# Attention and two feed-forward layers on one core: q in six loads per chunk, k and v loads and score products spread, a new cost table for the list scheduler

## The chip, the cores and the metric

The kernel runs on one core of one Trainium2 chip. The metric is device time in microseconds (us), the median of the runs shown, lower is better. One profiled execution, with its trace, stands beside the runs. In the trace PE is TensorE's matrix engine and PEld its weight loads, ACT is ScalarE, DVE is VectorE, POOL is GpSimd, and SP is the queue that issues every DMA of this kernel (SPq in the rows).

## The reference, cut to what matters

```python
# q, k, v: (4 batches, 12 heads, 448 tokens, 64); w_pre, w_post: (12, 12)
scores = scale * np.matmul(q, k.transpose(0, 1, 3, 2))
scores = np.einsum('bhij,hg->bgij', scores, w_pre)         # mixes the heads
attn = np.exp(scores - np.max(scores, axis=-1, keepdims=True))
attn = attn / (np.sum(attn, axis=-1, keepdims=True) + 1e-09)
attn = np.einsum('bhij,hg->bgij', attn, w_post)            # mixes them again
x = np.matmul(attn, v)                                     # -> (1792 tokens, 768)
h = x @ w_in                                               # 768 -> 2048, then a gate
x = gate(h) @ w_out                                        # 2048 -> 768
h = x @ w_in2                                              # 768 -> 1024
out = layer_norm(h * softmax(h)) * g_ln @ w_out2           # 1024 -> 768
```

## The kernel before

The attention is cut into 16 chunks: 4 batches, and in each batch 4 chunks of 110, 110, 110 and 118 tokens. A chunk has 11 or 12 groups of 10 tokens (`GR`), and two groups make a pair, so there are 180 groups and 90 pairs. The same steps run for each chunk:

- `load_q` (L262) brings the chunk's q of all 12 heads into one of two slots of `qb`, with two DMAs. `load_k` (L255) brings k of two heads, six loads for a batch, and `load_v` (L271) brings v in four loads for a batch. A k tile lives in the ring `kraw`, of 12 buffers.
- `qk` (L282), six times, makes the scores of two heads in two tiles of the PSUM ring `psa` (4 tiles). It is the "score product" of the title.
- `qk_evac` (L290), twelve times on ACT, copies one head's scores to a tile `s`, from a ring of 5.
- `remap` (L295), twelve DMAs issued by SP, moves a tile `s` so that in `sr` a group's 10 tokens of all heads lie on the partitions. The buffer of `s` is free again when its remap has landed.

For each pair of groups follow `pre` (L306, PE, mixes the heads), `rmax` (L311, DVE), `expo` (L316, ACT, the exponential), `guard`, `norm` and `wscale` (L323 and L331 on POOL, L327 on DVE, the divisor folded into the mixing weights `wr`), `post` (L345, PE, 64 matmuls, mixes and transposes) and two copies to `at` (L361 on ACT or L363 on DVE). After a chunk's last pair `av` (L374, PE) runs twice, a copy and an addition follow (L383, L389), and `store_x` (L393) writes to the scratch `xs`. When the last remap is done, SP begins to load the weights of the first feed-forward layer (L547); their conversion on DVE, ACT and POOL and the first matmuls overlap the end of the attention.

The program is written out once, in the order that a planner makes on the host (class `Order`). Every step is a task with an engine, an assumed duration, dependencies, buffers of rings and a priority in units of groups. The planner walks through time: of the tasks of an engine that could start, it takes the one with the lowest priority number:

```python
            t = min((t for t in avail[e] if ready(t) <= st), key=lambda t: (t.prio, t.i))
```

On the chip only the order on each engine is left of it: every engine works off its own row in that order and waits at the head of it for what the task needs. SP is such a row too: a remap whose `s` is not ready holds up every load behind it. The priorities come from the table `OFFS`, added to the first group of a chunk (`t0`) or of a pair (`p`): `qk0` and `qks` place the score products, `sq` the q loads, `sk` the k loads, `sv` the v loads, `pre`, `rmax`, `expo`, `post`, `av0` the steps of a pair. The list `gates` adds a lower bound: a load in it comes no earlier in the planner's order than the `pre` of a given pair (`marks`).

Of the kernel before, what the change touches and what calls it, by code (L numbers as in the profile page):

```python
# [17 lines left out]
H, S, D = 12, 448, 64  # L18
# [4 lines left out]
T0 = [0, 110, 220, 330]  # L23
NTOK = [110, 110, 110, 118]
JC, JP = 4, 112
OFFS = dict(split=-7.944, pre=0.954, rmax=-3.67, expo=-5.22, guard=-3.381, norm=-0.14, post=2.988, eh=-16.359, el=-2.885, av0=11.716, avs=2.48, sq=-16.055, exact=174, sld=1000, linact=(), wral=0, early=18, b_in=984, b_x=988, b_out=991, b_x1=998, lw=-90, shal=180, wrp=(), vlp=(),
   qk0=-13.451, qks=0.797, dmalat=2100, sk=-4.076, sv=-8.254, nv=1, svs=0.624,
   mw=-5, start=(('k', 0, 1), ('q', 0, 1), ('k', 1, 1), ('q', 1, 2), ('k', 2, 2), ('q', 3, 3), ('k', 4, 2)))


BUFS = dict(kraw=12, q=2, vv=2, s=5, sr=2, p=8, st=8, wr=6, x=3, psa=4, psb=4)
LAT_DMA = 2100
XPOOL = (0, 1, 'in', 'out')
SCALE = {}
# [164 lines left out]
def attention(nc, od, pl, q, k, v, w_pre, w_post, mask, xs):  # L199

    P = OFFS
    add = od.add
# [195 lines left out]
    gates, marks = [], []  # L398
# [8 lines left out]
    def make_av(i, b, c, t):  # L407
        for u in range(2):
            pr = t + P['av0'] + P['avs'] * u
            m = add("PE", 2260, pr, av, i, b, c, u, deps=evs[i] + vt_d[b], new=[r_psa, r_psa], use=[(r_vv, b)])  # L410
            a1 = add("Activation", 370, pr, av_copy, i, c, u, deps=[m], new=[r_x], use=[(r_psa, -1)])
            a2 = add("DVE", 410, pr, av_add, i, c, u, deps=[a1], use=[(r_x, -1), (r_psa, -2)])
            avs.setdefault(i, []).append(m)
            stores[b].append(od.dma("SP", 625, 630, pr, store_x, i, b, c, u, deps=[a2], use=[(r_x, -1)]))

    def make_two(two):
        p = two[0][3]
        rms = two[0][5] + two[1][5]
        m = add("PE", 754, p + P['pre'], pre, [(tt, i, g) for i, b, c, tt, g, _ in two], deps=[t_w] + rms + t_zs[0] + t_zs[1],
                new=[r_psb, r_psb], use=[(r_sr, i) for i in sorted({x[0] for x in two})])  # L420
        marks.extend([m, m])
        x1 = add("DVE", 531, p + P['rmax'], rmax, p, deps=[m], new=[r_st], use=[(r_psb, -2)])
        y1 = add("DVE", 531, p + 1 + P['rmax'], rmax, p + 1, deps=[m], use=[(r_st, -1), (r_psb, -1)])
        x2 = add("Activation", 611, p + P['expo'], expo, p, deps=[x1], new=[r_p], use=[(r_psb, -2), (r_st, -1)])
        y2 = add("Activation", 611, p + 1 + P['expo'], expo, p + 1, deps=[y1], new=[r_p], use=[(r_psb, -1), (r_st, -1)])
        x3 = add("Pool", 165, p + P['guard'] - 5, guard, p, deps=[x2, y2], use=[(r_st, -1)])
        x3 = add("DVE", 80, p + P['norm'], norm, p, deps=[x3], use=[(r_st, -1)])
        x4 = add("Pool", 350, p + P['norm'], wscale, p, deps=[x3], new=[r_wr], use=[(r_st, -1)])
        m = add("PE", 912, p + P['post'], post, p, deps=[x4], new=[r_psb, r_psb], use=[(r_p, -2), (r_p, -1), (r_wr, -1)])
        same = two[0][0] == two[1][0]  # L430
        ends = []
        for k, (i, b, c, tt, g, _) in enumerate(two[:1] if same else two):
            if g == 0:
                for j in (i - 2,):
                    busy[i] = avs.get(j, [])
            for r in range(2):
                eng = "Activation" if (p // 2 + r) % 2 in EV else "DVE"
                n = 2 if same else 1
                dur = 500 if same else 300
                e1 = add(eng, dur + (60 if eng == "DVE" else 0), p + P['el'], evac, p, eng, r, k, n, i, g,  # L440
                         deps=[m] + busy.get(i, []), use=[(r_psb, -2 + r)])
                evs.setdefault(i, []).append(e1)
            if tt + n - 1 == last[i]:
                ends.append((i, b, c, last[i] + 1))
        for e in ends:
            make_av(*e)
# [3 lines left out]
    for i, (b, c) in enumerate(chunks):  # L450
        t0 = t
        n = GR[c] * R
        last[i] = t + GR[c] - 1
        if i == 0:
            q0 = {}
            for what, h0, nh in P['start']:
                if what == 'k':
                    for p in range(h0, h0 + nh):
                        kt[b, p] = od.dma("SP", 450, 640, -100, load_k, b, p, new=[r_kraw])
                else:  # L460
                    a1 = od.dma("SP", 1250, nh * 400, -100, load_q, i, b, c, h0, nh,
                                **(dict(join=[r_q]) if h0 else dict(new=[r_q])))
                    for h in range(h0, h0 + nh):
                        q0[h] = a1
        else:
            a1 = od.dma("SP", 1250, 2000, t0 + P['sq'] - 3, load_q, i, b, c, 0, H // 2, new=[r_q])
            gates.append((a1, t0 + P['sq'] - 3))
            q0 = {p: a1 for p in range(H // 2)}
        rms = []
        for h in range(H):  # L470
            pr = t0 + P['qk0'] + P['qks'] * h
            if c == 0 and b and h % 2 == 0:
                kt[b, h // 2] = od.dma("SP", 450, 640, pr + P['sk'] - 2, load_k, b, h // 2, new=[r_kraw])
                gates.append((kt[b, h // 2], pr + P['sk'] - 2))
            if h % 2 == 0:
                a1 = add("PE", 754, pr, qk, i, b, c, h // 2, deps=[q0[h // 2], kt[b, h // 2]], new=[r_psa, r_psa],
                         use=[(r_q, i), (r_kraw, b * H // 2 + h // 2)])
            a2 = add("Activation", 424, pr, qk_evac, b, c, h, deps=[a1], new=[r_s], use=[(r_psa, -1 if h % 2 else -2)])
            rms.append(od.dma("SP", 625, 550, pr, remap, i, b, c, h, deps=[a2], use=[(r_s, -1)],
                              new=[] if h else [r_sr], join=[r_sr] if h else []))  # L480
        if c == 0:
            vt_d[b] = []
            for m in range(4):
                pr = t0 + P['sv'] + m
                a1 = od.dma("SP", 450, 960, pr - 2, load_v, b, m, **(dict(join=[r_vv]) if m else dict(new=[r_vv])))
                gates.append((a1, pr - 4 if b else t0 + m))
                vt_d[b].append(a1)
        for g in range(GR[c]):
            pend.append((i, b, c, t + g, g, rms))
            if len(pend) == 2:  # L490
                make_two(pend)
                pend = []
        t += GR[c]
    for x, slot in gates:
        if slot >= 0:
            x.issue.deps.append(marks[min(int(slot), len(marks) - 1)])
    late = list(od.tasks)
    early = [u for n in A_EARLY for us in rg[n].users for u in us]

# [522 lines left out]
```

## Time and profile before

| | |
|---|---|
| median of 3 runs | 1160.25 us (1158.41 to 1170.82) |
| profiled execution, device time | 1163.11 us |
| span of its trace | 1161.3 us |
| mean granted TensorE clock | 0.973 |
| PE busy over the span | 1080.2 us (93%) |
| DVE, ACT, POOL busy | 675.2, 523.2, 300.6 us |

The span is the time from the first to the last instruction of the profiled execution; 1.8 us of its device time lie outside. Busy times of different engines overlap. The attention fills the span up to about 390 us, with its last pairs mixed into the first matmuls of the feed-forward layer; the two layers fill the rest.

### The profile page before, as it was taken

The numbers are of one execution on the slowest core, as the hardware profiler recorded it, in microseconds if no ns is written. First come the engines' busy times: TensorE is split into PE (matmuls) and PEld (weight loads), VectorE is DVE, ScalarE is ACT, GpSimd is POOL, SyncE is SP. The second block draws the span as 40 slices with busy tenths as digits, with TensorE's granted clock in tenths as the row PEclk, the third lists the DMA queues.
The fourth block names the chain that finished last, engine by engine and source line by source line (L and its number), as shares of the span: only waits on it lengthen the run. The fifth ranks groups of instructions, "written<-read, shape, count | busy, mean of one in ns | idle before, by whom it ended". The sixth has DMA issues, their size and how long they took to land.

```text
span 1161.3 us, 31401 instructions
## 1 busy us (share of the span) xinstructions
PE 1080.2 (93%) x13528; PEld 918.0 (79%) x13528; DVE 675.2 (58%) x1078; ACT 523.2 (45%) x1053; POOL 300.6 (26%) x427
## 2 busy tenths in 40 slices
PE   5897998988897889999999899899999999999998
PEld 1475775766676668998989799798999898998988
DVE  0453554545454997488887778688866534243241
ACT  2775776867675656422233222232334232232232
POOL 3111110111111684243444344354510000000000
PEclk7998999999999899999999999899999999999999
DMA  5766457546646451241423232333222000000001
GB/s 144 202 180 182 126 164 204 158 140 179 183 137 203 124 181 65 73 136 55 139 79 128 82 109 97 107 107 112 82 86 93 26 14 28 28 14 28 28 14 41
DMA packets 84514, 124.20 MB, mean 107 GB/s; under 512 B 31544, under 2 KB 71960, under 8 KB 84376
## 3 DMA queue, kind: packets, MB, share of 16 engines
q1 hardware_dynamic: 84376, 122.20, 34.6%
q8 instruction: 106, 1.74, 0.7%
q14 instruction: 32, 0.26, 0.1%
HBM read 66.17 MB, written 17.30 MB: 72 GB/s over the span
## 4 chain that ended last, share of the span: by engine, by line
PE 64%; DVE 16%; DMA 8%; POOL 4%; issue 3%; ACT 3%; SPq 1%; ACTq 0%; POOLq 0%; DVEq 0%
PE ps_post L345 7%; DMA sr<-s 5%; PE ps_qk L282 5%; PE ps_pre L306 4%; PE ps_av L374 4%; PE ps_o L704 4%; PE ps_o L706 4%; PE ps_o L705 4%; PE ps_h L674 4%; PE ps_h L676 4%; PE ps_h L675 4%; PE ps_ot L904 3%; PE ps_ot L902 3%; PE ps_ot L903 3%; PE ps_h L842 3%
## 5 line engine op out<-in xcount | busy, mean ns | idle before, releaser
L345 PEld LDWEIGHTS ps_post<-wr,p 64*64 64x64 f32 x5760 | 115.2, 142 | 55.9 <-issue 42.2
L704 PE MATMUL ps_o<-g,wout 128*128 128x448 f32 x384 | 144.8, 377 | 14.6 <-DVE x2acc L714 12.0
L345 PE MATMUL ps_post<-wr,p 64*64 64x60 f32 x5760 | 121.9, 228 | 35.6 <-issue 19.3
L706 PE MATMUL ps_o<-g,wout 128*128 128x448 f32 x384 | 143.8, 375 | 0.0
L705 PE MATMUL ps_o<-g,wout 128*128 128x448 f32 x384 | 143.7, 374 | 0.0
L311 DVE TENSOR_REDUCE nm<-ps_pre 128x1 f32<-128x448 f32 x180 | 102.1, 618 | 60.5 <-PE ps_pre L306 58.9
L290 ACT ACTIVATE s<-ps_qk 119x448 f32<-119x448 f32 (+1 forms) x192 | 97.4, 550 | 69.4 <-DMA sr<-s 50.7
L316 ACT ACTIVATE p<-ps_pre,nm 128x448 f32<-128x448 f32 x180 | 112.3, 635 | 27.9 <-DVE nm L311 27.7
L282 PE MATMUL ps_qk<-kraw,qb 64*64 64x448 f32 (+2 forms) x768 | 109.0, 589 | 16.8 <-ACT s L290 9.5
L593 POOL TENSOR_TENSOR m<-m,v 128x768 f32<-128x768 f32 (+1 forms) x52 | 95.2, 1831 | 89.2 <-DVE v L575 76.8
L714 DVE TENSOR_TENSOR x2acc<-ps_o,x2acc 128x448 f32<-128x448 f32 x168 | 100.3, 616 | 21.8 <-PE ps_o L706 21.5
L565 ACT ACTIVATE v<-v,ebias 128x768 int32<-128x768 int32 (+1 forms) x52 | 46.1, 887 | 131.9 <-DVE v L561 131.8
L306 PE MATMUL ps_pre<-sr,wp 64*64 64x448 f32 (+1 forms) x720 | 94.8, 557 | 3.0 <-ACT s L290 1.0
L374 PEld LDWEIGHTS ps_av<-at,vv 64*64 64x64 f32 x2688 | 80.3, 133 | 18.9 <-issue 7.9
L704 PEld LDWEIGHTS ps_o<-g,wout 128*128 128x128 f32 x384 | 73.5, 191 | 24.9 <-DVE x2acc L714 14.9
L848 DVE TENSOR_REDUCE st<-ps_h 128x1 f32<-128x1024 f32 x14 | 17.1, 1225 | 128.7 <-PE ps_h L844 128.7
L374 PE MATMUL ps_av<-at,vv 64*64 64x110 f32 (+1 forms) x2688 | 84.8, 259 | 6.6 <-ACT s L290 2.5
L323 POOL TENSOR_SCALAR nm<-nm 128x2 f32<-128x2 f32 x90 | 18.6, 207 | 278.3 <-ACT p L316 277.8
L363 DVE COPY at<-ps_post 128x480 f32<-128x480 f32 (+1 forms) x98 | 59.4, 612 | 38.8 <-PE ps_post L345 38.1
L680 ACT ACTIVATE t<-ps_h,half 128x448 f32<-128x448 f32 x64 | 40.3, 629 | 91.3 <-PE ps_h L676 87.9
L706 PEld LDWEIGHTS ps_o<-g,wout 128*128 128x128 f32 x384 | 73.7, 192 | 7.4
L705 PEld LDWEIGHTS ps_o<-g,wout 128*128 128x128 f32 x384 | 73.7, 192 | 7.0
(110 smaller groups left out, 2302.9 us busy)
## 6 DMA issues: line engine op xcount, KB each, us to landing
sr<-s SPq DMA_DIRECT2D x144, 192.5 KB
raw<-in_moe_w_out_dram SPq DMA_DIRECT2D x24, 768.0 KB
raw<-in_moe_w_in_dram SPq DMA_DIRECT2D x16, 768.0 KB
sr<-s SPq DMA_DIRECT2D x48, 210.0 KB
raw<-in_moe_w_in_dram SPq DMA_DIRECT2D x12, 512.0 KB
kraw<-in_k_dram SPq DMA_DIRECT2D x24, 224.0 KB
out_dram<-ot SPq DMA_DIRECT2D x13, 384.0 KB
vv<-in_v_dram SPq DMA_DIRECT2D x12, 384.0 KB
```

The lines of the kernel that those rows point to most:

```text
L282: nc.tensor.matmul(out=qk_t[b, c, 2 * p + e][64 * j:at_], lhsT=qb[rows, i % 2, lo:hi], rhs=kraw_t[b, p][rows], start=True, stop=True,)
L290: nc.scalar.activation(out=s[:n], in_=qk_t.pop((b, c, h))[:n], func=AF.Copy, scale=0.125)
L306: nc.tensor.matmul(out=pre_t[t][o:o + 64], lhsT=wp[k_], rhs=sr[i % 2][k_, g, :], start=True, stop=True)
L311: nc.vector.tensor_reduce(nm_t[t // 2][:, 0, t % 2:t % 2 + 1], pre_t[t], axis=AX.X, op=ALU.max, negate=True)
L316: nc.scalar.activation(out=p, in_=pre_t.pop(t), func=AF.Exp, bias=nm[:, 0, e], accum_out=nm[:, 1, e])
L345: nc.tensor.matmul(out=ps[i][64 * j:64 * j + 64, e, m, :], lhsT=p[64 * i:64 * i + 64, x:x + 64], rhs=wr[64 * i:64 * i + 64, e], start=True ...
L374: nc.tensor.matmul(out=ps[r][64 * j:64 * j + 64, a, :n], lhsT=v_t[b][rows, m, (h0 + j) * D:(h0 + j + 1) * D], rhs=at[rows, i % 2, m, h0 + ...
L593: nc.gpsimd.tensor_tensor(out=m, in0=m, in1=vt.pop(key).bitcast(F32)[:, :n], op=ALU.mult)
L704: nc.tensor.matmul(out=ps, lhsT=wh, rhs=g[:, 0], start=(i == 0), stop=False)
L705: nc.tensor.matmul(out=ps, lhsT=wh, rhs=g[:, 1], start=False, stop=False)
L706: nc.tensor.matmul(out=ps, lhsT=wl, rhs=g[:, 0], start=False, stop=(i == 1))
L714: nc.vector.tensor_tensor(out=dst, in0=op.pop((u, m)), in1=dst, op=ALU.add)
```

## The change

- `load_q` is called six times per chunk, each for two heads (a pair of DMAs of one head's rows each), at priorities `sq + sqs * p`, where it was called once. The first chunk's loads are as they were.
- The k loads of later batches get priorities of their own, `sk + sks * p`, counted from the chunk's first group, and so do the v loads (`sv + svs * m` with a step of 2.5); the v loads of the first batch move to priorities 1 to 7.
- The score products join the list `gates`: product p of a chunk comes no earlier in the planner's order than the pair at `t0 + qg + qgs * p`.
- The ring `kraw` has 8 buffers for 12.
- The planner's durations change: a remap has 800 and 1300 ns (issue and transfer) for 625 and 550, a pair of q DMAs 1200 and 380 where the whole load had 1250 and 2000, k and v loads 500 and 720 or 1150 for 450 and 640 or 960, `av` 2320 for 2260, `post` 945 for 912, `wscale` 390 for 350, the copy after `av` 335 for 370. Several offsets in `OFFS` change with them.

No step of the computation is added or left out, and the instructions on PE, ACT, DVE and POOL are the same in number. SP issues 12 DMAs for a chunk's q where it issued 2.

```diff
-OFFS = dict(split=-7.944, pre=0.954, rmax=-3.67, expo=-5.22, guard=-3.381, norm=-0.14, post=2.988, ...
-   qk0=-13.451, qks=0.797, dmalat=2100, sk=-4.076, sv=-8.254, nv=1, svs=0.624,
+OFFS = dict(sqs=1.5, sks=-5.148, qg=-14.0, qgs=1.359, split=-7.944, pre=0.481, rmax=1.193, expo=-8.093, ...
+   qk0=-13.451, qks=0.569, dmalat=2100, sk=-25.042, sv=-9.216, nv=1, svs=2.5,
...
-BUFS = dict(kraw=12, q=2, vv=2, s=5, sr=2, p=8, st=8, wr=6, x=3, psa=4, psb=4)
+BUFS = dict(kraw=8, q=2, vv=2, s=5, sr=2, p=8, st=8, wr=6, x=3, psa=4, psb=4)
...
-            a1 = od.dma("SP", 1250, 2000, t0 + P['sq'] - 3, load_q, i, b, c, 0, H // 2, new=[r_q])
-            gates.append((a1, t0 + P['sq'] - 3))
-            q0 = {p: a1 for p in range(H // 2)}
+            q0 = {}
+            for p in range(H // 2):
+                pq = t0 + P['sq'] + P['sqs'] * p
+                q0[p] = od.dma("SP", 1200, 380, pq, load_q, i, b, c, p, 1, **(dict(join=[r_q]) if p else dict(new=[r_q])))
+                gates.append((q0[p].issue, pq))
...
-                kt[b, h // 2] = od.dma("SP", 450, 640, pr + P['sk'] - 2, load_k, b, h // 2, new=[r_kraw])
-                gates.append((kt[b, h // 2], pr + P['sk'] - 2))
+                pk = t0 + P['sk'] + P['sks'] * (h // 2)
+                kt[b, h // 2] = od.dma("SP", 500, 720, pk, load_k, b, h // 2, new=[r_kraw])
+                gates.append((kt[b, h // 2].issue, pk))
...
+                gates.append((a1, t0 + P['qg'] + P['qgs'] * (h // 2)))
...
-            rms.append(od.dma("SP", 625, 550, pr, remap, i, b, c, h, deps=[a2], use=[(r_s, -1)],
+            rms.append(od.dma("SP", 800, 1300, pr, remap, i, b, c, h, deps=[a2], use=[(r_s, -1)],
...
-                pr = t0 + P['sv'] + m
-                a1 = od.dma("SP", 450, 960, pr - 2, load_v, b, m, **(dict(join=[r_vv]) if m else dict(new=[r_vv])))
-                gates.append((a1, pr - 4 if b else t0 + m))
+                pr = t0 + P['sv'] + P['svs'] * m if b else 1 + 2 * m
+                a1 = od.dma("SP", 500, 1150, pr, load_v, b, m, **(dict(join=[r_vv]) if m else dict(new=[r_vv])))
+                gates.append((a1.issue, pr))
```

What the table and the gates do to the order is shown at three places. The first is SP's row at the start, from the first chunk's remaps (`sr<-s`) on; `qb` is q. Before:

```order
L295 DMA sr<-s 10x11x448 x5
L262 DMA qb<-in_q_dram 64x6x110 x2
L295 DMA sr<-s 10x11x448 x13
L271 DMA vv<-in_v_dram 128x768 x3
L271 DMA vv<-in_v_dram 64x768
L295 DMA sr<-s 10x11x448
```

After, on the same engine from the same remaps on:

```order
L295 DMA sr<-s 10x11x448 x5
L262 DMA qb<-in_q_dram 64x110 x2
L295 DMA sr<-s 10x11x448 x2
L262 DMA qb<-in_q_dram 64x110 x2
L295 DMA sr<-s 10x11x448 x3
L262 DMA qb<-in_q_dram 64x110 x2
L295 DMA sr<-s 10x11x448 x2
L262 DMA qb<-in_q_dram 64x110 x4
L295 DMA sr<-s 10x11x448
L262 DMA qb<-in_q_dram 64x110 x2
L295 DMA sr<-s 10x11x448 x3
L271 DMA vv<-in_v_dram 128x768
```

The pairs of q loads and the first batch's v loads now stand between the remaps. Up to the second chunk's last remap, the 24th, SP's row holds 4 DMAs for q before and 20 after.

The second place is SP's row where the first batch ends: the 12-group remaps (10x12x448) are those of its last chunk, and `kraw` is k of the second batch. Before:

```order
L295 DMA sr<-s 10x12x448 x4
L255 DMA kraw<-in_k_dram 128x448
L393 DMA xs<-x 128x3x110
L262 DMA qb<-in_q_dram 64x6x110 x2
L255 DMA kraw<-in_k_dram 128x448
L295 DMA sr<-s 10x12x448 x3
L255 DMA kraw<-in_k_dram 128x448
L295 DMA sr<-s 10x12x448
L393 DMA xs<-x 128x3x110
L255 DMA kraw<-in_k_dram 128x448 x2
L295 DMA sr<-s 10x11x448 x3
L255 DMA kraw<-in_k_dram 128x448
```

After, from the second batch's second k load on (its first stands three remaps ahead):

```order
L255 DMA kraw<-in_k_dram 128x448
L295 DMA sr<-s 10x12x448
L262 DMA qb<-in_q_dram 64x120 x2
L255 DMA kraw<-in_k_dram 128x448 x2
L295 DMA sr<-s 10x12x448 x3
L262 DMA qb<-in_q_dram 64x110 x2
L255 DMA kraw<-in_k_dram 128x448 x2
L393 DMA xs<-x 128x3x110
L262 DMA qb<-in_q_dram 64x110 x2
L295 DMA sr<-s 10x12x448 x2
L393 DMA xs<-x 128x3x110
L295 DMA sr<-s 10x12x448
```

Before, the last k load stood behind three remaps of the batch that needs it. Now all six stand ahead of the fifth remap of the last chunk of the batch before. The v loads, which began two remaps behind the last k load, now begin 13 remaps behind it.

The third place is ACT's row at the same boundary: `s<-ps_qk` is the evacuation of one head's scores, `p,nm<-ps_pre,nm` the exponential of one group, `at<-ps_post` a copy behind `post`. Before:

```order
L290 ACTIVATE s<-ps_qk 119x448 x2
L383 ACTIVATE x<-ps_av 128x3x110
L316 ACTIVATE p,nm<-ps_pre,nm 128x448
L361 ACTIVATE at<-ps_post 128x2x48x5
L316 ACTIVATE p,nm<-ps_pre,nm 128x448
L290 ACTIVATE s<-ps_qk 119x448 x3
L316 ACTIVATE p,nm<-ps_pre,nm 128x448 x4
L290 ACTIVATE s<-ps_qk 119x448
L383 ACTIVATE x<-ps_av 128x3x110
```

After:

```order
L316 ACTIVATE p,nm<-ps_pre,nm 128x448 x2
L361 ACTIVATE at<-ps_post 128x2x48x5
L290 ACTIVATE s<-ps_qk 124x448 x2
L361 ACTIVATE at<-ps_post 128x2x48x5
L290 ACTIVATE s<-ps_qk 124x448
L316 ACTIVATE p,nm<-ps_pre,nm 128x448 x2
L361 ACTIVATE at<-ps_post 128x2x48x5
L290 ACTIVATE s<-ps_qk 124x448 x2
L316 ACTIVATE p,nm<-ps_pre,nm 128x448 x2
L290 ACTIVATE s<-ps_qk 124x448
L383 ACTIVATE x<-ps_av 128x3x110
```

Where three evacuations stood in a row with four exponentials behind them, one or two evacuations now alternate with one pair's two exponentials.

## Rows read from the trace of the kernel before

**Rows 1.** Busy us (and instructions) of PE, PEld, DVE, ACT, POOL; PEclk, DMA share, GB/s.

```profile
30.00:390.00 360.00, 316.37 (x9284) 238.06 (x9279) 181.65 (x385) 257.09 (x650) 55.92 (x177) 0.96 0.60 169
```

**Rows 2.** PE's waits between 30 and 390 us: total us, times, longest.

```profile
PE ps_post L345 <- issue: 18.9, 17, 4.3
PE ps_post L345 <- ACT p L316: 13.5, 12, 3.7
```

**Rows 3.** PE's timeline at three batch boundaries: start, us; idle before in brackets.

```profile
99.68 0.86 PE L345 MATMUL ps_post<-wr,p 64*64 64x60 f32 x44 [1.60 <-issue]
...
104.58 1.73 PE L282 MATMUL ps_qk<-kraw,qb 64*64 64x448 f32 x16 [1.55 <-DMA sr<-s]
...
113.09 3.73 PE L345 MATMUL ps_post<-wr,p 64*64 64x60 f32 x126 [3.03 <-ACT p L316]
...
185.21 0.98 PE L282 MATMUL ps_qk<-kraw,qb 64*64 64x448 f32 x8 [1.63 <-DMA kraw<-in_k_dram]
...
203.94 0.33 PE L345 MATMUL ps_post<-wr,p 64*64 64x60 f32 x4 [3.50 <-ACT p L316]
...
300.13 0.33 PE L345 MATMUL ps_post<-wr,p 64*64 64x60 f32 x4 [3.72 <-ACT p L316]
```

**Rows 4.** The chain that ended last, start, us, what: the start and two boundaries.

```profile
14.29 3.43 DMA sr<-s
...
102.48 9.20 DMA sr<-s
...
290.47 8.25 DMA sr<-s
```

**Rows 5.** Busy time by stretch, columns as in rows 1, around the boundaries.

```profile
113.00:116.60 3.60, 3.46 (x124) 3.31 (x128) 1.31 (x4) 2.76 (x8) 1.16 (x4) 0.55 0.58 197
189.70:191.60 1.90, 1.90 (x134) 1.90 (x131) 0.82 (x2) 0.99 (x3) 0.94 (x3) 1.00 0.70 206
197.50:203.90 6.40, 2.72 (x88) 2.25 (x82) 1.75 (x4) 2.35 (x6) 0.00 (x0) 1.00 0.97 247
...
300.10:304.20 4.10, 3.88 (x132) 3.77 (x136) 1.40 (x4) 2.70 (x8) 1.16 (x4) 0.58 0.53 182
```

**Rows 6.** The chain again, where four steps follow one another without a gap.

```profile
250.03 0.93 PE ps_post L345 x64
250.96 1.51 PE ps_qk L282 x16
252.47 1.50 PE ps_pre L306 x16
253.97 2.22 PE ps_av L374 x84
```

**Rows 7.** SP's DMA issues by line: ns min/median/max, first and last start in us.

```profile
L295 SPq DMA_DIRECT2D sr<-s x192: 755/756/1972, 14.3 to 365.8; - x192
...
L262 SPq DMA_DIRECT2D qb<-in_q_dram x36: 582/658/1368, 1.2 to 336.0; - x36
...
L255 SPq DMA_DIRECT2D kraw<-in_k_dram x24: 385/492/756, 0.7 to 283.9; - x24
...
L393 SPq DMA_DIRECT2D xs<-x x32: 359/380/1458, 70.1 to 424.1; - x32
```

**Rows 8.** SP's timeline: one-head q loads, first five remaps, the 21st to 24th remap.

```profile
1.17 1.23 SPq L262 DMA_DIRECT2D qb<-in_q_dram  x2
...
14.29 4.33 SPq L295 DMA_DIRECT2D sr<-s  x5
...
39.47 6.11 SPq L295 DMA_DIRECT2D sr<-s  x4
```

**Rows 9.** SP's waits between 14 and 353 us: total us, times, longest.

```profile
SPq L295 <- ACT s L290: 52.3, 52, 3.3
SPq L295 <- PE ps_pre L306: 43.6, 14, 7.1
SPq L393 <- DVE x L389: 37.0, 16, 6.1
```

More of the change, by code (lines that the diff above doesn't have):

```diff
@@ L25 @@
 JC, JP = 4, 112
-OFFS = dict(split=-7.944, pre=0.954, rmax=-3.67, expo=-5.22, guard=-3.381, norm=-0.14, post=2.988, eh=-16.359, el=-2.885, av0=11.716, avs=2.48, sq=-16.055, exact=174, sld=1000, linact=(), wral=0, early=18, b_in=984, b_x=988, b_out=991, b_x1=998, lw=-90, shal=180, wrp=(), vlp=(),
-   qk0=-13.451, qks=0.797, dmalat=2100, sk=-4.076, sv=-8.254, nv=1, svs=0.624,
+OFFS = dict(sqs=1.5, sks=-5.148, qg=-14.0, qgs=1.359, split=-7.944, pre=0.481, rmax=1.193, expo=-8.093, guard=-3.381, norm=0.182, post=2.988, eh=-16.359, el=-2.885, av0=13.489, avs=2.424, sq=-20.655, exact=174, sld=1000, linact=(), wral=0, early=18, b_in=984, b_x=988, b_out=991, b_x1=998, lw=-90, shal=180, wrp=(), vlp=(),
+   qk0=-13.451, qks=0.569, dmalat=2100, sk=-25.042, sv=-9.216, nv=1, svs=2.5,
    mw=-5, start=(('k', 0, 1), ('q', 0, 1), ('k', 1, 1), ('q', 1, 2), ('k', 2, 2), ('q', 3, 3), ('k', 4, 2)))
-BUFS = dict(kraw=12, q=2, vv=2, s=5, sr=2, p=8, st=8, wr=6, x=3, psa=4, psb=4)
+BUFS = dict(kraw=8, q=2, vv=2, s=5, sr=2, p=8, st=8, wr=6, x=3, psa=4, psb=4)
 LAT_DMA = 2100
@@ L409, in make_av @@
             pr = t + P['av0'] + P['avs'] * u
-            m = add("PE", 2260, pr, av, i, b, c, u, deps=evs[i] + vt_d[b], new=[r_psa, r_psa], use=[(r_vv, b)])
-            a1 = add("Activation", 370, pr, av_copy, i, c, u, deps=[m], new=[r_x], use=[(r_psa, -1)])
+            m = add("PE", 2320, pr, av, i, b, c, u, deps=evs[i] + vt_d[b], new=[r_psa, r_psa], use=[(r_vv, b)])
+            a1 = add("Activation", 335, pr, av_copy, i, c, u, deps=[m], new=[r_x], use=[(r_psa, -1)])
             a2 = add("DVE", 410, pr, av_add, i, c, u, deps=[a1], use=[(r_x, -1), (r_psa, -2)])
@@ L427, in make_two @@
         x3 = add("DVE", 80, p + P['norm'], norm, p, deps=[x3], use=[(r_st, -1)])
-        x4 = add("Pool", 350, p + P['norm'], wscale, p, deps=[x3], new=[r_wr], use=[(r_st, -1)])
-        m = add("PE", 912, p + P['post'], post, p, deps=[x4], new=[r_psb, r_psb], use=[(r_p, -2), (r_p, -1), (r_wr, -1)])
+        x4 = add("Pool", 390, p + P['norm'], wscale, p, deps=[x3], new=[r_wr], use=[(r_st, -1)])
+        m = add("PE", 945, p + P['post'], post, p, deps=[x4], new=[r_psb, r_psb], use=[(r_p, -2), (r_p, -1), (r_wr, -1)])
         same = two[0][0] == two[1][0]
@@ L495, in attention @@
         if slot >= 0:
-            x.issue.deps.append(marks[min(int(slot), len(marks) - 1)])
+            x.deps.append(marks[min(int(slot), len(marks) - 1)])
     late = list(od.tasks)
```

## The prediction, made before the changed kernel ran

> **What bounds the kernel now.** I read the busy times by stretch first: which engine is near full, and where. From 30 to 390 us PE is busy 316.4 of 360 us, ACT 257.1, DVE 181.7, and the DMA engines 0.60 of the time [rows 1]. Only the attention's order changes, so I take the rest of the span as it is. PE is idle for 43.6 of those 360 us, and that is what another order can win.
>
> Next I read PE's waits there. Two kinds lead: 18.9 us in 17 waits ahead of `post` for nothing that the profile shows ("issue"), and 13.5 us in 12 waits of `post` for the exponential on ACT [rows 2]. The first kind has no cause in these rows. The timeline shows where the second sits: the long ones are at the three places where a batch ends. There PE is idle 1.60, 1.55 and 3.03 us (first boundary), 1.63 and 3.50 us (second) and 3.72 us (third), 15.0 us in all [rows 3].
>
> Then the chain, for what stands behind them. At the first boundary it runs through a remap that needs 9.20 us from issue to landing, at the third through one of 8.25 us; the first remap of the program, with an idle queue, needs 3.43 us [rows 4]. The stretch ahead of the second boundary's wait shows why: the DMA engines are 0.97 busy at 247 GB/s [rows 5], because k, v and the whole q load stand close together in SP's row. A slow remap holds a tile of `s`, ACT's next evacuation waits for that tile, and ACT works in order, so the exponentials behind the evacuations wait too (ACT's order before: three evacuations, then four exponentials). `post` waits for them.
>
> Behind each of these waits the granted clock is down: 0.55 at 113 us and 0.58 at 300 us, where PE had been idle 3.03 and 3.72 us; that lies close to the lower of its two levels, 1.2 GHz against 2.4. In the undisturbed stretch at 189.7 us it is 1.00 [rows 5].
>
> **The change part by part.** The sum is made against the profiled execution (span 1161.3 us, device time 1163.1) and taken off the median, 1160.25; the execution is 0.25% above the median, less than what I argue about.
>
> *k and v loads spread, q in pieces: less crowding.* If no remap meets a crowd any more, the 15.0 us go. With them goes the slow clock: 124 matmuls of `post` take 3.46 us of busy time at 0.55 and 134 take 1.90 us at full clock [rows 5], so a pair of `post` costs some 1.7 us more there, 1.9 at the third. Part of that overlaps the weight loads, so I take 1.2 us at each boundary, 3.6 in all, bounds 0 and 5. Together 18.6 us.
>
> *q in pieces: SP's row.* A pair of one-head q loads took 1.23 us at the start, 0.64 each with its gap [rows 8]; a six-head load takes 0.66 [rows 7]. So the issue costs the same whatever it moves, and a chunk's q costs 12 x 0.64 = 7.7 us of SP where it cost 1.4. Five remaps issued without a wait took 4.33 us, 0.87 each [rows 8]. A plain chunk now needs 12 x 0.87 + 7.7 + 2 stores of 0.38 and a gap [rows 7] = 19.0 us of SP; k adds 6 x 0.54 = 3.2 and v 4 x 0.54 = 2.2 (v taken like k, 0.49 and a gap [rows 7]). Over the whole attention, with 15 of the 16 chunks loading q this way: 14.3 (start) + 192 x 0.87 + 15 x 7.7 + 34 x 0.54 + 28 x 0.43 = 327 us. The last remap is issued at 365.8 us now [rows 7], so SP has 39 us left for its own waits, 2.4 us a chunk.
>
> PE's pace to compare: `post` 0.93 us a pair, `pre` 0.75, a score product 0.75, half of `av` 2.22 [rows 6]; 5.6 pairs, 6 products and two `av` make 18.3 us a chunk without any idle time. SP and PE would both be full, and the last remap at 365.8 us says that a chunk takes nearer 22 now. So in a plain chunk SP keeps up, and at the two chunks around a boundary (22.2 and 21.2 us) it hardly does.
>
> *What comes late instead.* At the first boundary PE's new order has, from the first product of the batch's last chunk to the `pre` that needs its last remap, 7 products, 7 `post`, 3 `av` and 5 `pre`: 22.2 us by rows 6. SP in the same stretch: 12 remaps, 12 q loads, 4 k loads, 2 stores = 21.2 us, with 1.4 us ahead of it until the first evacuation is done and 3.4 us behind it for the landing [rows 4]: 26.0 us. That `pre` would wait 3.8 us. At the other two boundaries the same count of PE's row gives 24.6 and 23.0 us against 26.0, so 1.4 and 3.0. Sum 8.2 us if PE runs without a gap; PE is 12% idle now [rows 1], and at 10% more time per stretch the three come to 1.6, 0 and 0.7, 2.3 us. I take 5.
>
> *The start.* Here SP is issuing all the time. The second chunk's last remap is the 24th, issued by 45.6 us now [rows 8]. With 20 q loads and 3 v loads ahead of it: 14.3 + 24 x 0.87 + 20 x 0.64 + 3 x 0.54 = 49.6 us. That is 4.0 us later at most, but the q load that used to follow the fifth remap in one piece is thinned out, and PE has one `post` more behind it by then. Cost between 0 and 4, taken 1.
>
> *The "issue" waits.* The new order sometimes has three `post` pairs in a row (384 weight loads and matmuls) and `av` and `post` alternating, denser than before. Since I can't name their cause, I take the 17 waits as unchanged: 0, bounds -6 (a third go) and +6.
>
> *8 k buffers for 12.* A k load of the next batch now waits until the product four places back in the last chunk has run. SP waits for it at the head of its row with remaps behind it; two products stand next to each other in PE's order at that place, so about 0.8 us, and it lies in the 5 above. The durations of `av`, `post` and the copies only move the planner's own clock.
>
> Sum: -18.6 + 5 + 1 + 0 = -12.6 us, 1147.7: I say **1148**.
>
> **A rule that speaks against the change.** A q piece moves a sixth of the old load and costs the same 0.6 us to issue. The Trainium skill, "DMA: Bandwidth & Descriptors", section "Rules for kernel authors", advises to join many small transfers into one large one, since a small one is mostly overhead. By that rule the six pieces only lose; rows 7 and 8 agree for the issue, and what it would make of the time is the second rival.
>
> **The rivals.** *The loss only moves.* SP's lateness costs what the crowding cost: the `pre` at each boundary waits 8.2 us in all, the start costs 4, and the denser stretches 4 more of "issue". Then -18.6 + 16 = -2.6, **1158**. For it speaks that SP goes from some 233 us (15 x 1.4 for q in the sum above) to 327 us of issuing; against it that now the remaps, not the issues, take the 8 to 9 us [rows 4].
>
> *SP sets the pace, slower than before.* SP works in order, and each remap, store and load at its head may wait. Three rows alone give 133 us of waits, 8.3 us a chunk [rows 9]. What decides is how much of them stays: up to 2.4 us a chunk the last remap is no later than now, at 3.5 us it comes 16 x 1.1 = 18 us later, and everything behind it too: **1178**. For it: a store waits for DVE behind `av`, and more DMAs now stand between it and the next remap. Against it: most of the waits are SP being early, which a fuller row shrinks by itself. The page "Perfetto Trace Analysis" of the Trainium skill, section 'What "DMA-bound" means', lists a solid row of DMA slices on the issuing queue as a bound of its own; that is this case, and no row before shows it, since SP is not solid there.
>
> *All of it goes.* Nothing comes late (5 and 1 become 0), and a third of the "issue" waits, 6 us, go with the slower burst of DMA: -24.6, **1136**.
>
> *The change doesn't do what it says.* The order shows that k, v and q are spread; I give it nothing.
>
> **How the numbers follow.** Forecast 0.42 (1142 to 1154), the loss moves 0.27, SP sets the pace 0.17, all goes 0.14. A measurement of this kernel can tell about 1% from no change, so the lines are at 1148.6 and 1171.9. The forecast straddles the upper one: 0.25 of its 0.42 lie under 1148.6 and 0.17 above. Faster: 0.25 + 0.14 + 0.02 of the second case = 0.41. Slower: 0.17. Same: 0.42. The range leaves out a tenth at each end: down to 1134, into the last case, and up to 1172, where the case of SP begins to count. The case of the likeliest sign, faster or unchanged, runs from 1134 to 1160.
>
> **What would show it.** Right: the waits of `post` for ACT at the ends of the batches are under 1.5 us each, no remap on the chain takes over 6 us, the clock in the stretches behind is near 1.00, SP issues some 320 us of the first 360, and the last remap is issued near 353 us. Wrong by the first rival: `pre` waits for a remap that was issued late, with SP solid ahead of it. Wrong by the second: the last remap comes after 366 us, and SP's waits per chunk are over 2.4 us. The start is read from the 24th remap, between 45.6 and 49.6 us. What I can't foresee is where the "issue" waits fall: four more of 3 to 4 us would undo the gain without any of the above being wrong.

## The result and the profile after

| | before | after |
|---|---|---|
| median | 1160.9 us (4 runs) | 1179.0 us (4 runs, 1171.01 to 1179.7) |
| profiled execution, device time | 1163.11 us | 1179.12 us |
| span of its trace | 1161.3 us | 1177.3 us |
| mean granted TensorE clock | 0.973 | 0.978 |

The changed kernel is slower: 1.0145 times the time of before, 95% interval 1.0103 to 1.0187, some 17 us. The prediction of 1148 us lies 31 us too low, and the time is above the range's upper end of 1172. Here and below a ratio is taken against the kernel before in the same rounds, whose median moves from 1160.9 to 1165.6 us between rounds; the ratios can be compared, the medians of different rounds less well.

Busy time of the changed kernel in the stretch of [rows 1], with the same columns:

```profile
30.00:390.00 360.00, 311.75 (x8950) 225.31 (x8954) 172.90 (x369) 245.11 (x631) 48.64 (x170) 0.97 0.57 158
```

Every engine got less done in these 360 us: 8950 matmuls where it was 9284, 631 instructions on ACT for 650. No engine took over as the bound, and the DMA engines are less busy than before (0.57 for 0.60). All of them are idle for longer.

PE's waits in the changed kernel between 30 and 410 us (us in total, times, longest), for [rows 2]; the stretch is 20 us longer, as the attention is:

```profile
PE ps_post L345 <- issue: 12.6, 15, 2.0
PE ps_av L374 <- issue: 10.7, 10, 2.5
PE ps_pre L306 <- DMA qb<-in_q_dram: 6.9, 2, 4.8
PE ps_pre L306 <- issue: 4.0, 1, 4.0
...
PE ps_pre L306 <- DMA sr<-s: 2.7, 2, 1.7
...
PE ps_post L345 <- ACT p L316: 1.4, 7, 0.2
```

The waits that the forecast was about are gone: `post` waits 1.4 us for ACT, never more than 0.2 at a time, where it was 13.5 and up to 3.7. In their place `pre` waits for DMAs (6.9 + 2.7 us) and `av` waits 10.7 us without a visible cause. (`pre` reads no q. The release named `qb` is the trace's inference; what `pre` needs is the last remap of its chunk, which stands among the q pieces in SP's row.) The longest of them is at the start: PE waits 4.84 us there, and `pre` begins at 32.48 us; before, PE had score products to fill that time, and `pre` began at 31.69.

PE's timeline of the changed kernel, idle time before in brackets, for [rows 3]:

```profile
32.48 1.77 PE L306 MATMUL ps_pre<-sr,wp 64*64 64x448 f32 x8 [4.84 <-DMA qb<-in_q_dram]
...
248.22 1.34 PE L306 MATMUL ps_pre<-sr,wp 64*64 64x448 f32 x10 [1.66 <-DMA sr<-s]
...
296.65 0.59 PE L306 MATMUL ps_pre<-sr,wp 64*64 64x448 f32 x2 [2.04 <-DMA qb<-in_q_dram]
```

The chain that ended last (start, us, what), for [rows 4]:

```profile
50.82 4.93 DMA sr<-s
...
211.23 6.04 DMA sr<-s
...
239.97 8.21 DMA sr<-s x2
```

No single remap takes 9.20 or 8.25 us any more; the longest on the chain is 6.04 us. The chain goes through remaps in plain chunks, as it did before (six of them, 3.36 to 4.91 us, between 130 and 356 us). The two from 239.97 us take 3.93 and 4.28 us and end in PE's wait of 1.66 us at 248.22: they are not slow, but late. What stands around them in SP's row is the next reading: SP's timeline there (start, us, what, how many).

```profile
230.02 0.60 SPq L262 DMA_DIRECT2D qb<-in_q_dram  x1
230.72 1.75 SPq L295 DMA_DIRECT2D sr<-s  x2
232.57 0.44 SPq L393 DMA_DIRECT2D xs<-x  x1
233.07 1.66 SPq L262 DMA_DIRECT2D qb<-in_q_dram  x2
234.83 1.77 SPq L295 DMA_DIRECT2D sr<-s  x2
236.65 3.21 SPq L262 DMA_DIRECT2D qb<-in_q_dram  x4
239.97 2.60 SPq L295 DMA_DIRECT2D sr<-s  x3
242.62 1.17 SPq L262 DMA_DIRECT2D qb<-in_q_dram  x2
243.89 0.82 SPq L295 DMA_DIRECT2D sr<-s  x1
244.82 1.55 SPq L393 DMA_DIRECT2D xs<-x  x2
246.64 3.81 SPq L295 DMA_DIRECT2D sr<-s  x4
```

Each row merges issues with the gaps between them. Taken one by one, the 24 issues and up to 0.2 us of the gap behind each fill 19.6 of the 20.4 us from 230.02 to 250.45; the longest gap is 0.75 us, between the two stores. SP hardly rests: this is the solid row that the prediction's second rival speaks of, and no k or v load is in it. By the prices of the prediction (0.87, 0.64 and 0.43) the twelve remaps, nine q pieces and three stores would have filled 17.5.

SP's issues by line (ns min/median/max, first and last start in us), for [rows 7]:

```profile
L295 SPq DMA_DIRECT2D sr<-s x192: 755/822/1457, 14.3 to 389.2; - x192
...
L262 SPq DMA_DIRECT2D qb<-in_q_dram x186: 466/589/1622, 1.2 to 368.2; - x186
```

The issue of a q piece takes SP 589 ns at the median where a load of six heads took 658, and there are 150 more of them, 88 us by the median. The last remap is issued at 389.2 us, 23.4 later than before. SP's waits between 14 and 353 us, for [rows 9]:

```profile
SPq L295 <- ACT s L290: 33.4, 51, 2.3
SPq L295 <- ACT p L316: 25.8, 42, 1.2
SPq L295 <- ACT at L361: 11.5, 16, 2.0
SPq L295 <- ACT x L383: 6.2, 10, 0.9
SPq L393 <- DVE x L389: 3.8, 4, 1.4
```

A remap's wait for a place in `sr` (43.6 us before, for `pre`) has left the list, and the stores' wait for DVE fell from 37.0 to 3.8 us: there SP had been early, and a fuller row used the time up. The waits for ACT that are left must be read beside the timeline. The five rows make 80.7 us, but SP's issues leave far less room: added up over its timeline from 14.29 us to the last remap's end at 390, the issues, and up to 0.2 us of each gap between two of them, fill 351.3 of 375.7 us; what longer gaps have beyond that is 24.4. So most of these waits end while the DMA ahead is still being issued, and cost nothing.

### The profile page after: what moved, and what is told of

Same layout as the page of the kernel before. It is cut to its first block, busy times and chain, and to the rows that moved or that the text cites. A ratio compares the mean times of both kernels' runs of the same rounds, so it can differ in the third digit from the quotient of the medians.

```text
span 1177.3 us, 31649 instructions
## 1 busy us (share of the span) xinstructions
PE 1084.2 (92%) x13528; PEld 913.6 (78%) x13528; DVE 680.1 (58%) x1078; ACT 520.5 (44%) x1053; POOL 300.8 (26%) x427
## 4 chain that ended last, share of the span: by engine, by line
PE 60%; DVE 17%; DMA 7%; issue 5%; POOL 5%; ACT 4%; SPq 2%; ACTq 0%; POOLq 0%; DVEq 0%
PE ps_post L345 7%; PE ps_av L374 5%; PE ps_pre L306 4%; DMA sr<-s 4%; PE ps_o L708 3%; PE ps_ot L908 3%; PE ps_ot L906 3%; PE ps_ot L907 3%; PE ps_h L846 3%; PE ps_qk L282 3%; PE ps_h L847 3%; PE ps_h L678 3%; PE ps_o L710 3%; PE ps_o L709 3%; PE ps_h L848 3%
## 5 line engine op out<-in xcount | busy, mean ns | idle before, releaser
L345 PE MATMUL ps_post<-wr,p 64*64 64x60 f32 x5760 | 121.4, 223 | 26.5 <-issue 12.6
L282 PE MATMUL ps_qk<-kraw,qb 64*64 64x448 f32 (+2 forms) x768 | 117.5, 579 | 16.0 <-ACT s L290 8.9
L306 PE MATMUL ps_pre<-sr,wp 64*64 64x448 f32 (+1 forms) x720 | 106.9, 571 | 20.2 <-DMA qb<-in_q_dram 6.9
L718 DVE TENSOR_TENSOR x2acc<-ps_o,x2acc 128x448 f32<-128x448 f32 x168 | 100.2, 614 | 20.3 <-PE ps_o L710 20.0
L374 PE MATMUL ps_av<-at,vv 64*64 64x110 f32 (+1 forms) x2688 | 87.6, 264 | 12.7 <-issue 10.7
L306 PEld LDWEIGHTS ps_pre<-sr,wp 64*64 64x64 f32 (+1 forms) x720 | 39.8, 139 | 49.9 <-issue 22.9
```

The costliest lines, as they stand in the source:

```text
L282: nc.tensor.matmul(out=qk_t[b, c, 2 * p + e][64 * j:at_], lhsT=qb[rows, i % 2, lo:hi], rhs=kraw_t[b, p][rows], start=True, stop=True,)
L306: nc.tensor.matmul(out=pre_t[t][o:o + 64], lhsT=wp[k_], rhs=sr[i % 2][k_, g, :], start=True, stop=True)
L345: nc.tensor.matmul(out=ps[i][64 * j:64 * j + 64, e, m, :], lhsT=p[64 * i:64 * i + 64, x:x + 64], rhs=wr[64 * i:64 * i + 64, e], start=True ...
L374: nc.tensor.matmul(out=ps[r][64 * j:64 * j + 64, a, :n], lhsT=v_t[b][rows, m, (h0 + j) * D:(h0 + j + 1) * D], rhs=at[rows, i % 2, m, h0 + ...
L718: nc.vector.tensor_tensor(out=dst, in0=op.pop((u, m)), in1=dst, op=ALU.add)
```

## The experiments

Two theories stood against each other. **A**: the 150 added issues take SP's time and the remaps come late. **B**: the new order itself (pair offsets, gates for the score products, places of the loads) costs the time on PE and ACT. A third question came with the first answers: where did the forecast gain go? Lines of the kernels that add a helper are moved by up to 11 from those of before.

**1. The old order with twelve q issues.** The kernel before, whose q load issues six pairs at its old place:

```diff
+    def load_q6(i, b, c):
+        for p in range(H // 2):
+            load_q(i, b, c, p, 1)
-            a1 = od.dma("SP", 1250, 2000, t0 + P['sq'] - 3, load_q, i, b, c, 0, H // 2, new=[r_q])
+            a1 = od.dma("SP", 1250, 2000, t0 + P['sq'] - 3, load_q6, i, b, c, new=[r_q])
```

> The order of the kernel before on every engine; only at each q load's place SP issues twelve one-head DMAs in a row instead of two. Theory A (SP's issuing time sets the new pace: 150 more DMAs at 0.64 us are 96 us of SP): 1168 to 1180 us, with SP's waits between 14 and 353 us falling from some 196 to about 100 us. Theory B (the issues fit into SP's idle time, the new order of products and pair steps on PE, ACT and DVE costs the time): 1157 to 1166 us, last remap within 4 us of 365.8.

Measured: 1235.86 us, ratio 1.0602 (1.0544 to 1.066). The issues alone, in the old order, cost 6%, far more than A had said. ACT's largest wait in this kernel between 30 and 410 us, and the remaps on SP:

```profile
ACT s L294 <- DMA sr<-s: 107.0, 64, 8.1
```

```profile
L299 SPq DMA_DIRECT2D sr<-s x192: 755/756/1702, 14.3 to 445.1; - x192
```

Before, ACT's evacuations waited 36.4 us in 32 waits for remaps to free their tile, here 107.0 in 64, up to 8.1 us. Twelve issues in one block stand ahead of remaps that ACT needs; the last remap comes at 445.1 us. SP's row is not full here: up to that remap the issues, with up to 0.2 us of each gap, fill 348.9 of 431.6 us. So the sum of the issues doesn't explain these 6%; the place of the block must cost as well.

**2. The new order with two q issues.** The changed kernel, in which the first of the six places issues the whole load and the other five nothing. The order of everything else is that of the changed kernel:

```diff
+    def load_q1(i, b, c, p):
+        if p == 0:
+            load_q(i, b, c, 0, H // 2)
-                q0[p] = od.dma("SP", 1200, 380, pq, load_q, i, b, c, p, 1, ...
+                q0[p] = od.dma("SP", 1200, 380, pq, load_q1, i, b, c, p, ...
```

> The changed kernel's order on every engine; only all of a chunk's q comes with two six-head DMAs at the place of the first piece, and the five other places issue nothing. Theory A (SP's issuing sets the pace): the time falls below the kernel before, 1145 to 1160 us, since k and v are still spread. Theory B (the order of products and pair steps costs it): stays at 1170 to 1180 us, with DVE's waits for the copy behind av and ACT's waits for the row maximum as long as now (48.9 and 45.2 us).

Measured: 1167.68 us, ratio 1.000 (0.9968 to 1.0032; the kernel before had 1165.55 in these rounds). The time lies between the ranges of A and B: the whole loss is gone, so B falls as an explanation of it, but the gain that A expected as well did not come. PE's waits in this kernel between 30 and 390 us:

```profile
PE ps_post L349 <- issue: 11.7, 14, 1.8
PE ps_av L378 <- issue: 10.6, 9, 3.2
PE ps_post L349 <- DVE at L367: 3.7, 5, 0.8
...
PE ps_post L349 <- ACT p L320: 1.7, 9, 0.2
```

The long waits for ACT are gone here too, and no wait of PE for a DMA is left; yet by its median the kernel is no faster than before. (The profiled execution is the fastest of ten, 1158.13 us, so its trace looks better than the median.) The last remap is issued at 370.4 us. Beside it the loss can be found on PE: here 9411 matmuls are done between 30 and 390 us and PE is idle for 39.1 us; in the changed kernel it takes until 410 us to do 9428, and PE is idle for 53.1. Of the 14.0 us more, 11.1 are waits for DMAs (6.9, 2.7 and, ahead of a score product, 1.5); at the start, where the changed kernel waits 4.8, kernel 2 waits 2.8 for nothing visible.

**3. The issues without their bytes.** As in 2, but the other five places issue a pair of DMAs of one element for each partition (0.2 KB) into a tile that nothing reads:

```diff
+        for e in range(2):
+            nc.sync.dma_start(
+                out=dm[e * D:(e + 1) * D, 6 * i + p:6 * i + p + 1],
+                in_=q[b, c, :, 2 * p + e:2 * p + e + 1],
+            )
```

> The changed kernel's order; all of q comes at the first piece's place with two DMAs, and at each of the five other places SP issues two DMAs that move one element per partition to a tile that nothing reads, so that SP's issues are as many as in the change while q lies there early. If SP's issuing time is what costs: 1173 to 1182 us. If late pieces of q cost: 1160 to 1170 us.

Measured: 1180.56 us, ratio 1.0138 (1.0104 to 1.0173): the loss is back, with q as early and as whole as in 2. SP's issues in this kernel:

```profile
L273 SPq DMA_DIRECT2D dm<-in_q_dram x150: 471/589/1658, 22.0 to 367.3; - x150
...
L306 SPq DMA_DIRECT2D sr<-s x192: 755/822/1652, 14.3 to 386.1; - x192
```

A DMA of 0.2 KB holds SP for the same 589 ns as a q piece of 27.5 KB. So it is neither the bytes nor q that comes late, but SP's time.

**4. The q pieces issued by POOL.** The changed kernel with `nc.gpsimd` in place of `nc.sync` for the pieces.

> The changed kernel with the same order; the q pieces are issued from POOL's queue instead of SP's, at the same places. If SP's issuing time is what costs: 1155 to 1168 us, as with two DMAs per chunk (ratio 1.000). If the pieces cost as transfers or by coming late: 1173 to 1182 us. POOL may lose some time itself to twelve issues per chunk, which would show in its waits ahead of wscale.

Measured: 1169.48 us, ratio 1.0034 (1.0003 to 1.0064), 1.5 us above the range given for it. Most of the loss goes when the same 180 pieces leave SP's row; an issue takes 523 ns (median) of POOL's. The profiled execution, 1174.56 us, is above the median and doesn't show the gain: its last remap comes at 384.4 us, though SP's issues fill only 213.3 of 370.9 us up to there. So a late last remap alone is no proof of a full row; what delayed it in this execution wasn't found. The Trainium skill, "DMA: Bandwidth & Descriptors", section "Issuing engines are not separate DMA queues", says that initiating DMAs on several engines only saves the sequencer's time, "which is usually small relative to the DMA itself". It does save just that; here it is about 1% of the kernel.

**5. Only k and v spread.** The kernel before with its q load untouched and k and v at the changed kernel's places (12 k buffers stay):

```diff
-                kt[b, h // 2] = od.dma("SP", 450, 640, pr + P['sk'] - 2, load_k, b, h // 2, new=[r_kraw])
+                pk = t0 - 25.042 - 5.148 * (h // 2)
+                kt[b, h // 2] = od.dma("SP", 500, 720, pk, load_k, b, h // 2, new=[r_kraw])
...
-                pr = t0 + P['sv'] + m
+                pr = t0 - 9.216 + 2.5 * m if b else 1 + 2 * m
```

> The kernel before with the k and v loads alone at their new places (their planner durations too); q in one load, 12 k buffers, products and pair steps as before. If the crowding of k, v and q at the batch ends was worth what the prediction took (15.0 us of waits and 3.6 us of slow clock): 1140 to 1150 us, and the waits of post for ACT at the three batch ends under 1.5 us each. If those waits only move to other places once loads move: 1156 to 1166 us.

Measured: 1160.05 us, ratio 0.9964 (0.9935 to 0.9993), the only version with full remaps whose interval lies below 1. It is the second of the two cases that were expected, not the gain of the prediction. PE's waits in it between 30 and 390 us:

```profile
PE ps_post L345 <- issue: 27.0, 22, 3.8
PE ps_pre L306 <- DMA sr<-s: 3.5, 1, 3.5
PE ps_post L345 <- ACT p L316: 3.0, 10, 0.8
```

The waits for ACT fell from 13.5 to 3.0 us, and the issue waits of `post` rose from 18.9 to 27.0.

**6. k and v spread, the start left alone.** In 5 the new places put two k loads and the first v loads among the first remaps. Here k is at `t0 - 30 + 2.5 * p`, and the first batch's v at its old places.

> The kernel before with k of the later batches some 30 to 17 groups ahead of the batch and v behind its first groups, spread as in the change; the first batch's loads and the whole start stay as before, q in two DMAs, 12 k buffers, and nothing else changes. If the spread itself is worth 9 to 10 us behind the start (12th pre pair to the 90th: 316.7 us against 327.0 in the run with spread loads) and the rest of its gain was lost to loads among the first remaps: 1147 to 1155 us. If the waits at the batch ends only scatter: 1157 to 1165 us.

Measured: 1161.38 us, ratio 0.9996 (0.9966 to 1.0027), again the second case. `post` waits 3.1 us for ACT, 23.0 for "issue", and `av` 5.9 for "issue" (1.4 before). The boundary waits went again, and again nothing was won.

**7 and 8. Short remaps.** To see what the slow remaps are worth at all, and whether the issue waits come from DMA traffic, from the second batch on the remaps move 64 of 448 columns. The rest of the work runs on old scores. 7 is the kernel before with this edit, 8 is kernel 5 with it:

```diff
-            out=sr[i % 2][pad + h:pad + H * R:H, :GR[c], :], in_=s_t.pop((b, c, h))[64 - n:64 + n]
+            out=sr[i % 2][pad + h:pad + H * R:H, :GR[c], :S if i < 4 else 64],
+            in_=s_t.pop((b, c, h))[64 - n:64 + n, :S if i < 4 else 64]
```

> The kernel before, in which the remaps from the second batch on move only the first 64 of 448 columns, so that the rest of the work runs on old scores (the output is not the reference's). No instruction is added or left out and no order changed; SP issues as many DMAs. It asks whether PE's waits that the trace puts down to issue come from the DMA traffic. Before, they are 9.9 us of post and 1.4 of av between 130 and 370 us, with the DMA engines 0.58 busy. If traffic is their cause (contention theory): the DMA share falls below 0.25 and the issue waits in that stretch fall under 4 us; together with the waits of post for ACT (9.0 us, which should go too as no remap is slow) the time falls by 12 to 18 us, to 1142 to 1150. If their cause lies in PE's own order and not in the traffic (rival): the issue waits stay at 8 to 17 us, and only the waits for ACT go: 1150 to 1158.

> The kernel that only spreads the k and v loads, again with remaps of 64 of 448 columns from the second batch on (the output is not the reference's). With full remaps its issue waits of post between 130 and 370 us were 17.4 us in 17 waits, and post waited 2.8 us for ACT. Contention theory: under 4 us of issue waits, and a time within 3 us of the same edit of the kernel before. Rival (the waits belong to PE's order, or PE runs into another limit as soon as it gains): 12 us or more of issue waits remain, and the time stays near 1155 to 1160.

Measured: 1130.72 us, ratio 0.9742 (0.968 to 0.9805), and 1131.8, 0.974 (0.9683 to 0.9796). Kernel 7 is below every number that either theory gave; kernel 8 is within 3 us of it, as the contention theory had said. Kernel 7 between 130 and 370 us, busy time and ACT's wait for remaps:

```profile
130.00:370.00 240.00, 222.94 (x6978) 173.57 (x6968) 138.79 (x285) 185.70 (x469) 49.55 (x134) 0.98 0.34 87
```

```profile
ACT s L290 <- DMA sr<-s: 8.5, 7, 3.1
```

The same two of the kernel before, in the same stretch:

```profile
130.00:370.00 240.00, 214.62 (x6432) 165.96 (x6436) 119.90 (x260) 173.65 (x441) 33.66 (x116) 0.98 0.58 162
```

```profile
ACT s L290 <- DMA sr<-s: 27.0, 26, 3.8
```

ACT's wait for remaps falls from 27.0 to 8.5 us, and PE gets 8% more matmuls done in the stretch. The remaps' own transfer is worth 2.6%: SP issues as many of them, at the same 756 ns. With it cut, spreading k and v is worth nothing more (0.9742 and 0.974).

For the issue waits the whole stretch from 30 to 390 us has to be read, since the same work comes earlier in the faster kernels: the wait of 4.0 us that ends at 348.38 us in kernel 7 ends at 377.65 in the kernel before (4.3). Kernel 7, then kernel 8:

```profile
PE ps_post L346 <- issue: 12.4, 15, 4.0
```

```profile
PE ps_post L346 <- issue: 12.6, 19, 4.8
```

With full remaps it is 18.9 us in the kernel before [rows 2] and 27.0 in kernel 5. So `post`'s issue waits fall by a third and by half when the remaps are short, and what kernel 5 had more than the kernel before is gone; some 12 us stay. Neither theory holds whole: a part of these waits hangs on the remaps' transfers, a part doesn't. Whether that first part comes from the DMA traffic (87 for 162 GB/s) or from remaps that land sooner, these two runs can't tell apart.

**9. Old pair offsets.** The changed kernel with `pre`, `rmax`, `expo`, `norm`, `av0` and `avs` of before.

> The changed kernel planned with the old offsets of the pair steps and of av (pre, rmax, expo, norm, av0, avs); q in six pieces, k and v loads, product gates and durations stay new. Theory A: stays at 1172 to 1182 us. Theory B in the form that these offsets do it (row maxima and the addition behind av block DVE's row): falls to 1155 to 1167 us, DVE's wait for the copy behind av from 48.9 to under 20 us.

Measured: 1175.37 us, ratio 1.0081 (1.0048 to 1.0114).

**10. No gate for the products.** The changed kernel without the line that adds the score products to `gates`.

> The changed kernel without the lower bound on the score products; all else as in the change, planned anew. Theory A: stays at 1172 to 1182 us. Theory B in the form that the spread products do it (their evacuations and remaps come late, one product between any two pair steps): falls to 1155 to 1167 us, the last product of a chunk earlier and the last remap near 370 us or before.

Measured: 1178.38 us, ratio 1.0108 (1.0065 to 1.0151). Both intervals overlap the changed kernel's; by the ratios the offsets would carry 0.6% of the loss and the gate 0.4%, and neither is settled. In both the q pieces still stand in SP's row, and the last remap comes at 381.8 and 388.4 us.

**11 and 12. New plans.** In 11 the changed kernel is planned anew with q as one load of 1400 and 2300 ns and the old pair offsets. In 12 kernel 2 is planned anew with the first batch's v at its old places.

> The changed kernel planned with q in one load (1400 and 2300 ns) at the first piece's priority, and with the old offsets of the pair steps and av; k and v spread, product gates, 8 k buffers and the other new durations stay. If SP's issuing is all that is wrong with the change and the rest is worth what was forecast: 1143 to 1153 us. If the rest is worth nothing: 1158 to 1166 us.

> The changed kernel planned as it is, with the first batch's v loads at their old places and all of a chunk's q issued with two DMAs at the first piece's place. If SP's issues and the loads among the first remaps are what the change lost: 1148 to 1156 us, with the 12th pre pair near 72 us instead of 77. If the new order of products and pair steps costs by itself: 1160 to 1168 us, as without this edit (ratio 1.000).

Measured: 1169.6 us, ratio 1.0062 (1.0032 to 1.0092), and 1170.8, 1.0085 (1.0058 to 1.0112). Both lie above every range that was given. Kernel 11, planned for the loads that it issues, is no faster than kernel 2, which is planned for six pieces that it doesn't issue. In kernel 12 other places of four v loads lose 0.85% through the plan that follows from them. So moves of this size can come from the plan alone, and kernels 9 and 10 don't rise above that. Kernels 2, 3 and 4 keep the plan of the changed kernel, and the cause of the loss rests on them.

## Why the prediction was wrong

Two terms of the sum failed, and together they make nearly all of the miss of 31 us: the gain of 18.6 us, of which kernel 2 shows nothing, and the cost of SP's row, taken at 6 us and measured at 16.8.

**The first step that failed** is "So in a plain chunk SP keeps up". From it came +5 and +1 us for late remaps, taken at boundaries and at the start alone. Measured between the changed kernel and the same order with two q issues, the added issues cost 1.45%, 16.8 us. The second rival, with a chance of 0.17, had the mechanism. Half of its sign came (the last remap after 366 us: 389.2), the other half, over 2.4 us of SP's waits a chunk, did not (1.5, below), and its 1178 us came near the 1179.0 in part by luck, as its terms were off both ways.

What was wrong in that step is the price of the issues. Added up over SP's timeline of the changed kernel from 14.29 us to the last remap, each with the gap behind it (up to 0.2 us), the mean costs are:

| | count | predicted, us | measured, us | difference in all |
|---|---|---|---|---|
| remap | 192 | 0.87 | 0.91 | 8 |
| q piece | 180 | 0.64 | 0.75 | 20 |
| store | 26 | 0.43 | 0.66 | 6 |
| k, v load | 34 | 0.54 | 0.69 | 5 |

Together with the 14.3 us ahead of the first remap they make 365.6 us where the prediction had 327, and 365.6 is where the last remap stood before (365.8). The 39 us of room for SP's own waits were not there at all; the 24.4 us of real waits that were left, 1.5 a chunk, came on top, and 365.6 + 24.4 is the last remap's end at 390. The rival had reached its 18 us from 2.4 us of room and 3.5 of waits a chunk; the runs gave none and 1.5. The prices came from a pair of issues in an idle queue and from medians. Issues scatter upwards: the q pieces have a median of 589 ns, a mean of 682 and a longest of 1622, and a sum over 180 of them goes by the mean. The trace of the kernel before had these prices: added up in the same way, its remaps cost 0.91 us, its q loads 0.80, its stores 0.63 and its k and v loads 0.67. With them the sum would have been some 373 us, past the 365.8. "Most of the waits are SP being early, which a fuller row shrinks by itself" was right, but no use without the room.

**The start** was sized at 0 to 4 us, with the 24th remap issued between 45.6 and 49.6 us. In SP's timeline of the changed kernel it stands here (start, us):

```profile
50.82 1.21 SPq L295 DMA_DIRECT2D sr<-s  x1
```

It ended at 52.03, 6.4 us later than before. SP's row from the first remap to this one has no gap over 0.45 us; it took 37.7 us where the sum had 35.3.

**The second step that failed** is "If no remap meets a crowd any more, the 15.0 us go". The waits went, the time did not. The waits of `post` for ACT shrank in every kernel that spreads k and v, from 13.5 to between 1.4 and 4.9 us. But without the cost of SP that came to 0.4% (4 us) in kernel 5 and to nothing that can be told from zero in kernels 2 and 6. Their traces show what stands there instead: "issue" waits of `post` and `av`, 28.8 us in kernel 5 and 28.9 in kernel 6 where before has 20.3 (18.9 and `av` 1.4), and in kernel 2 22.3 us of them, with waits of `post` and `pre` for DVE (3.7 and 2.3 us) and of `post` for POOL (3.4), of which before has only 0.7. The prediction took those of `post` as unchanged with bounds of 6; with `av` they rose by up to 8.6. It also named them as the way in which a gain could be undone, and so it was in kernels 5 and 6. Kernels 7 and 8 show that a part of them goes when the remaps are short; what else causes them, and why they grew, stays open.

**The slow clock** of 3.6 us: the windows behind the three boundaries of the changed kernel show it gone at two of them (columns as in [rows 1]):

```profile
109.80:118.00 8.20, 7.36 (x236) 5.30 (x235) 4.53 (x10) 5.16 (x15) 1.15 (x4) 1.00 0.67 191
...
207.00:216.00 9.00, 7.53 (x300) 6.40 (x304) 3.90 (x9) 6.75 (x17) 1.73 (x6) 1.00 0.73 205
...
296.60:304.00 7.40, 7.35 (x109) 4.40 (x111) 3.17 (x7) 4.59 (x12) 1.15 (x4) 0.77 0.52 140
```

It is 1.00 behind the first two and 0.77 behind the third, where PE had just idled 2.04 us for a late remap. In kernel 5, where other waits came in place of those for ACT, it is 0.95 over 30 to 390 us where it was 0.96: nothing was won back there.

**The late remaps at the boundaries**, taken at 5 us: at the third, `pre` waits 2.04 us (forecast 0.7 to 3.0); around the other two (100 to 135 and 195 to 225 us) PE waits for no DMA itself, though at the second the chain runs through the remap of 6.04 us and on over ACT to a wait of `pre` of 1.3 us. So the boundaries were priced too high. The mistake was to look for lateness only where the loads crowd; SP's row was solid in plain chunks.

**The rule** of the Trainium skill, "DMA: Bandwidth & Descriptors", section "Rules for kernel authors", that small transfers be joined, in the prediction an argument of the second rival, is borne out in the form that kernel 3 gives it: the issue costs 589 ns whether it moves 27.5 KB or 0.2.

## What to carry to other kernels

When a change cuts a DMA in pieces, add up the issuing row as one would an engine, with the mean cost of an issue in a busy stretch (mean, not median, and gap included), and set the sum against the time at which the row's last needed issue stands now. Read a queue's waits beside its timeline, for they can overlap the issue ahead of them. And before a stall is counted as a gain, ask what stands behind it: here 15 us of visible waits at three places won 4 us in one kernel and nothing in two others, while the remaps' transfers, cut short, were worth 30. When waits of two kernels are compared, take the stretch in which they do the same work, not the same microseconds.

## What the runs showed of the hardware

- An issue on SP costs 589 ns (median) for 27.5 KB and for 0.2 KB alike, 658 where mostly 165 KB are moved; on POOL 523.
- A remap's issue took 756 ns at the median in every kernel in which q wasn't spread over SP's row, and in kernel 1, where the pieces stood in one block; it took 822 or 823 where single pairs alternate with remaps (after, kernels 3, 9 and 10). With the gap behind it (up to 0.2 us) the mean is 0.91 us before and after alike, so the shift of the median costs the row nothing that shows; where it comes from wasn't tried.
- PE's waits without a visible cause ("issue"), 2.5 us (kernel 1) to 27.0 (kernel 5) ahead of `post` between 30 and 390 us, grew in kernels 5 and 6 as the waits for ACT went, and fell when the remaps moved a seventh of their bytes (18.9 to 12.4 us, and 27.0 to 12.6). What sets the rest wasn't found.
